# A block-sparse attention and gated FFN kernel whose instruction order is recomputed at build time: new planner prices, DMA as a planned resource, other key rows, mask rows by copies

## The chip, the cores and the metric

The kernel runs on one core of one Trainium2 chip. The metric is the time of one execution on the device in microseconds (us). A time is compared with a time, a profile with a profile; the profile's span is the time from the first to the last instruction.

## The reference

Attention over 4 batches, 8 heads, 768 positions and a head size of 64, with a mask on blocks of 32 positions, then an FFN with a three-tap convolution as gate:

```python
scores = scale * np.matmul(q, k.transpose(0, 1, 3, 2))
# visible: neighbouring blocks, first and last block row and column, 3 sampled key blocks per query block
scores = np.where(mask, scores, -1000000000.0)
attn = softmax(scores)                      # written out in the reference
x = np.matmul(attn, v)                      # (4, 768, 512) after joining the heads
h = np.maximum(x @ w_in, 0.0)               # (4, 768, 1024)
conv_out[s] = sum(conv_w[k] * h[s + k - 1] for k in range(3))
out = (h / (1.0 + np.exp(-conv_out))) @ w_out
```

The sampled blocks are an input, so all blocks are computed and the mask comes in as 24 more rows of the contraction: the query side holds a large negative number for each block that it may not see, the key side holds a one for the block that it belongs to. The softmax takes no maximum; the sum comes from a column of ones beside v.

## The kernel before, in words

**Units.** The 32 heads are 16 pairs P, four to a batch. The queries of a batch are cut in two halves, so there are 8 halves n. A half of four pairs is 18 *units* of eight 128x128 score blocks: TensorE fills one score tile `st` (L578), ScalarE takes the exponential into `pt` (L587), TensorE multiplies by v into `av` (L610). After a pair's last unit VectorE normalizes into `xtok` (L541, L542) and SyncE issues a DMA transpose into `xT` (L550). 144 units in all.

**FFN.** For each half: eight FFN1 blocks (L671, four matmuls of 384 columns into a `mix` tile), each followed by a relu into `hE` (VectorE L683 or ScalarE L681); for every two blocks GpSimd copies the edges for the taps (L696 to L702), VectorE makes three products (L710) in three slots of `m` and two sums (L718), ScalarE the tanh (L731), VectorE adds one (L734) and forms the gate `gT` (L737). Three out blocks (L640, eight matmuls of 512 columns) follow, each with an eviction into `o2s` (L650) and a store. The last column of a batch's first half waits for the second half and is patched in (L749 to L755).

**Loads.** Pair 0 comes by SyncE in fp32 (L286, staged in `o2s`) and is cast by VectorE (L474). All other q and k loads (`qk_loads`, L413) and all v loads (`v_load`, L428) are cast by the DMA and issued by GpSimd (POOL), with rows of three positions, 768 bytes; the two weight matrices are one load each (L393, L395). Pairs below `NPE = 4` are transposed by TensorE (L450) and copied out of PSUM by VectorE (L458) into the slots `et` and `ot`; the others by SyncE's DMA transposes from `nat` (L493), with an SBUF copy `ot<-et` and a mask copy `et<-msk` behind. There are six slots, three `nat` buffers and two `vn` buffers. The mask rows are built once: GpSimd forms block indicators (`bblk`, L312, L315), VectorE the visibility table from the sampled blocks (L320 to L335), TensorE multiplies the two (L344, L345); SyncE copies the rows to the other slots (L286). The conv weights come by three strided loads (L388).

**The order.** Nothing above is issued in program order. Every step is an `Op` with a price for each engine that may run it, its dependencies, buffers, and a due time made from `T(u)`, the planned start of unit u. `Scheduler.run` repeatedly takes the op that can start first (ties by due time) and puts it on its engine; the order so found is emitted, and each engine then runs its own list in order, waiting on semaphores. A DMA has a constant latency (2 to 3.8 us, the weights 12 and 14) and takes no other DMA's time. `FLEX = 1.0` keeps a relu or an eviction on VectorE unless VectorE would be a microsecond later than ScalarE. FFN work of half n is due from `T(18 (n + 1)) + 5`, its out blocks from 0.75 of a half later.

Of the kernel before, what the change touches and what calls it, by code (L numbers as in the profile page):

```python
# [48 lines left out]
FLEX = 1.0  # L49
LAT = {"PE": 0.22, "ACT": 0.20, "DVE": 0.15, "POOL": 0.20, "SP": 0.0}  # L50


class Scheduler:
# [21 lines left out]
    def run(self):  # L75
        free = {"PE": 0.0, "ACT": 0.0, "DVE": 0.0, "POOL": 0.0, "SP": 0.0}
# [10 lines left out]
        while left:  # L87
            still = []
            for o in blocked:
                r = o.earliest  # L90
                ok = True
                for d in o.deps:
                    r = max(r, d.end + (self.out_lat(d) if d.eng not in o.alts or len(o.alts) > 1
                                        or d.lat is not None else 0.0))
# [62 lines left out]
def kernel(  # L157
# [11 lines left out]
    nc = tc.nc  # L169
# [10 lines left out]
    NPE = 4  # L180
# [19 lines left out]
    NVN = 2  # L200
    vn_t = many(NVN, [128, 4, 192], BF16, "vn")
    NNAT = 3
    nat_t = many(NNAT, [128, 2, 2, 2, 192], BF16, "nat")
    MSK = sb.tile([88, 2, 2, 3, 128], BF16, tag="msk", name="msk")
    NPT = 5
    pt_t = many(NPT, [128, 1024], BF16, "pt")
    NXK = 3
    xtok_t = many(NXK, [128, 3, 2, 64], BF16, "xtok")
    rcp_t = many(NXK, [128, 2, 3], FP32, "rcp")
    NXT = 3  # L210
    xT_t = many(NXT, [128, NFC, 384], BF16, "xT")
    NHE = 3
    hE_t = many(NHE, [128, NFFC, 640], BF16, "hE")
    NCV = 3
    m_t = many(NCV, [128, 3, 2, 384], BF16, "m")
    tn_t = many(NCV, [128, 2, 384], BF16, "tn")
    NGT = 3
# [4 lines left out]
    NOS = 4  # L222
    o2s_t = many(NOS, [128, DM], FP32, "o2s")
    qf = [o2s_t[x][:, 0:384].rearrange("p (g c) -> p g c", g=2) for x in range(4)]
    winb = sb.tile([128, NFC, DFF], BF16, tag="winb", name="winb")
    woutb = sb.tile([128, NFFC, DM], BF16, tag="woutb", name="woutb")
    cw0 = sb.tile([128, 3, NFFC], FP32, tag="cw0", name="cw0")
    cw = sb.tile([128, 3, NFFC], FP32, tag="cw", name="cw")
    ident = sb.tile([128, 128], BF16, tag="ident", name="ident")
    warm = sb.tile([128, 512], BF16, tag="warm", name="warm")  # L230
    bblk = sb.tile([NB, 6, 128], BF16, tag="bblk", name="bblk")
    sbi = sb.tile([NB, 6], I32, tag="sbi", name="sbi")
# [19 lines left out]
    def t_act(n):  # L252
        return 0.147 + n / 1200.0

    def t_dps(n):
        return 0.14 + n / 960.0

    def t_d4(n):
        return 0.08 + n / 3840.0

    def t_d2(n):
        return 0.08 + n / 1920.0


    T0, PACE0, PACE1 = 7.0, 1.03, 1.2
# [3 lines left out]


    op = sc.op
    w0 = op({"DVE": 0.3}, lambda e: nc.vector.memset(warm, 0.0), -10)
    i_mem = op({"DVE": 0.1}, lambda e: nc.vector.memset(ident, 0.0), -9)
    b_mem = op({"DVE": 0.25}, lambda e: nc.vector.memset(bblk, 1.0), -9)
    a_mem = op({"DVE": 0.1}, lambda e: nc.vector.memset(A, 1.0), -8)
    r_mem = op({"DVE": 0.1}, lambda e: nc.vector.memset(row23, 1.0), -8)

    def warm_mm(e):
        nc.tensor.matmul(out=mix_t[1], lhsT=warm[:, 0:128], rhs=warm, start=True, stop=True)

    last = w0
    for x in range(7):
        last = op({"PE": 0.43}, warm_mm, -10, [last])

    def dma_h(dst, src):
        return lambda e: nc.sync.dma_start(out=dst, in_=src)  # L286

    def nat_src(t, b, h):
        return t[b, h].rearrange("(g p c) d -> p g (c d)", g=2, p=128)

    hw_q0 = op({"SP": 0.45}, dma_h(qf[0], nat_src(q, 0, 0)), -10, lat=2.2)
    hw_k0 = op({"SP": 0.45}, dma_h(qf[1], nat_src(k, 0, 0)), -9, lat=2.2)
    sb_ld = op({"SP": 0.45}, lambda e: nc.sync.dma_start(out=sbi, in_=sampled_blocks.bitcast(I32)),
               -8.5, lat=2.0)
    hw_q1 = op({"SP": 0.45}, dma_h(qf[2], nat_src(q, 0, 1)), -8, lat=2.5)
    hw_k1 = op({"SP": 0.45}, dma_h(qf[3], nat_src(k, 0, 1)), -8, lat=2.5)

    i_sel = op({"POOL": 0.3}, lambda e: nc.gpsimd.affine_select(
        out=ident, in_=ident, compare_op=ALU.not_equal, fill=1.0, base=0,
        pattern=[[-1, 128]], channel_multiplier=1), -9, [i_mem])  # L300
    col = op({"POOL": 0.2}, lambda e: nc.gpsimd.iota(colidx_i, pattern=[[1, NB]], base=0,
                                                      channel_multiplier=0), -8.9)
    a1 = op({"POOL": 0.24}, lambda e: nc.gpsimd.affine_select(
        out=A, in_=A, compare_op=ALU.is_ge, fill=0.0, base=1, pattern=[[-1, NB]],
        channel_multiplier=1), -8.8, [a_mem])
    a2 = op({"POOL": 0.24}, lambda e: nc.gpsimd.affine_select(
        out=A, in_=A, compare_op=ALU.is_ge, fill=0.0, base=1, pattern=[[1, NB]],
        channel_multiplier=-1), -8.7, [a1])
    r1 = op({"POOL": 0.24}, lambda e: nc.gpsimd.affine_select(
        out=row23, in_=row23, compare_op=ALU.is_ge, fill=0.0, base=-(NB - 1), pattern=[[0, NB]],  # L310
        channel_multiplier=1), -8.6, [r_mem])
    b1 = op({"POOL": 0.83}, lambda e: nc.gpsimd.affine_select(  # L312
        out=bblk, in_=bblk, compare_op=ALU.is_ge, fill=0.0, base=0,
        pattern=[[384, 2], [1, 3], [3, 128]], channel_multiplier=-32), -8.5, [b_mem])
# [10 lines left out]
    a3 = op({"DVE": 0.5}, a_edges, -7, [a2, r1])  # L325
    c1 = op({"DVE": 0.15}, lambda e: nc.vector.tensor_copy(out=colidx, in_=colidx_i), -7, [col])
# [11 lines left out]
    a4 = op({"DVE": 1.0}, a_rand, -9.5, [a3, c1, sb_ld])  # L338
# [3 lines left out]
    def w24(e):  # L342
        w = st_t[b_w.index]
        nc.tensor.matmul(out=w[0:NB, 0:384], lhsT=aadd, rhs=bblk[:, 0:6:2, :], start=True, stop=True)  # L344
        nc.tensor.matmul(out=w[0:NB, 512:896], lhsT=aadd, rhs=bblk[:, 1:6:2, :], start=True, stop=True)  # L345

    wmm = op({"PE": 0.7}, w24, -9, [a4, b2], alloc=b_w)

    def q_rows(dst, off):
        def fn(e):  # L350
            w = st_t[b_w.index]
            nc.scalar.copy(out=dst[64:88, 0, 0].rearrange("p c s -> p (c s)"),
                           in_=w[0:NB, off:off + 384])
        return fn

    qm_e = op({"ACT": 0.47}, q_rows(ET[0], 0), -9, [wmm], uses=[b_w])
    qm_o = op({"ACT": 0.47}, q_rows(OT[0], 512), -8.9, [wmm], uses=[b_w])

    def k_rows(dst, par):
        return lambda e: nc.vector.tensor_copy(  # L360
            out=dst[64:88, 1], in_=bblk[:, par:6:2, :].unsqueeze(1).broadcast_to([NB, 2, 3, 128]))

    km_e = op({"DVE": 0.3}, k_rows(ET[0], 0), -7.5, [b2])
    km_o = op({"DVE": 0.3}, k_rows(OT[0], 1), -7.5, [b2])
    qm_e1 = op({"DVE": 0.2}, lambda e: nc.vector.tensor_copy(out=ET[0][64:88, 0, 1], in_=ET[0][64:88, 0, 0]),
               T(0), [qm_e])
    qm_o1 = op({"DVE": 0.2}, lambda e: nc.vector.tensor_copy(out=OT[0][64:88, 0, 1], in_=OT[0][64:88, 0, 0]),
               T(0), [qm_o])
    msk = op({"DVE": 0.5}, lambda e: nc.vector.tensor_copy(out=MSK[64:88], in_=ET[0][64:88]),
             T(2), [qm_e1, km_e])  # L370
    o_mask, e_mask = {0: qm_o1}, {0: qm_e1}
    for s in range(1, NSLOT):
        if s < NPE:
            e_mask[s] = op({"SP": 0.45}, dma_h(ET[s][64:88], ET[0][64:88]), T(0) + s, [qm_e1, km_e], lat=2.0)
        o_mask[s] = op({"SP": 0.45}, dma_h(OT[s][64:88], OT[0][64:88]), T(0) + s, [qm_o1, km_o], lat=2.0)

    v_one = {}
    for s in range(NSLOT):
        v_one[s] = op({"DVE": 0.1}, lambda e, s=s: nc.vector.memset(VT[s][:, :, :, 64:65], 1.0), -5 + s)
    he_z = {}  # L380
    for s in range(NHE):
        def z(e, s=s):
            nc.vector.memset(hE_t[s][:, :, 639:640], 0.0)
        he_z[s] = op({"DVE": 0.2}, z, T(2))

    def cw_ld(e):
        for kk in range(3):
            nc.sync.dma_start(out=cw0[:, kk, :], in_=moe_conv_w[kk].rearrange("(ffc p) -> p ffc", p=128))  # L388

    cwl = op({"SP": 1.5}, cw_ld, T(8), lat=4.0, earliest=T(7))  # L390
    cw_op = op({"DVE": 0.1}, lambda e: nc.vector.tensor_scalar(out=cw, in0=cw0, scalar1=2.0, scalar2=None,
                                                                op0=ALU.mult), T(14), [cwl])
    win_ld = op({"POOL": 0.85}, lambda e: nc.gpsimd.dma_start(  # L393
        out=winb, in_=moe_w_in.rearrange("(fc p) ff -> p fc ff", p=128)), T(6), lat=12.0)
    wout_ld = op({"POOL": 0.85}, lambda e: nc.gpsimd.dma_start(  # L395
        out=woutb, in_=moe_w_out.rearrange("(ffc p) o -> p ffc o", p=128)), T(9), lat=14.0)


    first_u = [18 * (2 * (P // 4)) + (P % 4) * 4.5 for P in range(NP)]
    slot_b = [Buf(P_slot) for _ in range(NP)]  # L400
    slot_first = {}
    qk_ready = {}
    v_ready = {}

    def qk_loads(P):
# [401 lines left out]
```

## Time and profile before

| what | before |
|---|---|
| runs, us | 279.02, 275.28, 278.64; median 278.64 |
| the profiled execution, us | 277.88 |
| its span, us | 276.2 |
| its mean granted TensorE clock | 0.91 |
| TensorE busy, us | 213.5 |
| VectorE busy, us | 201.4 |
| ScalarE busy, us | 168.9 |
| GpSimd busy, us | 72.1 |
| DMA | 67778 packets, 30.35 MB |

How to read it: PE is TensorE, DVE VectorE, ACT ScalarE, POOL GpSimd, SP SyncE; "q" behind a name is the engine's queue or sequencer. A busy figure is a union of instruction durations; matmuls overlap, so their pitch is read from the start times of neighbours. A row of groups reads: line, engine, operation, out<-in with shapes, count | busy us, mean ns | idle time before it and what ended it. A row of waits reads: who <- for whom: us in total, times, longest. A row of the timeline: start, us, engine, line, operation, count, idle time before and its releaser. A row of windows: stretch, length, then busy us and instructions of PE, weight loads, DVE, ACT and POOL, granted clock, DMA share (1.00 is 16 engines busy; queues overlap, so it may be more) and GB/s.

### The profile page before, as it was taken

The page shows a single profiled execution, that of the slowest core. Times are in us where ns is not written, and L with a number is a line of the kernel's source. Part 1 is how long each engine was busy: PE and PEld are TensorE (multiplying, and loading weights), DVE is VectorE, ACT ScalarE, POOL GpSimd, SP SyncE. Part 2 cuts the span into 40 slices and gives each one's busy share as a digit, 9 for nine tenths or more (in the row PEclk, how much of TensorE's full clock was granted, in tenths as well). Part 3 has the DMA queues.
Part 4 walks back from the last instruction along what each step waited for, and adds up shares of the span by engine and source line. Part 5 has one row for each costly group of instructions (what it writes and reads, how often), then busy time and mean ns, then how long its engine had stood idle before and what let it go on. Part 6 is the DMA issues. An engine that isn't in the chain of part 4 may idle for free.

```text
span 276.2 us, 6428 instructions
## 1 busy us (share of the span) xinstructions
PE 213.5 (77%) x2503; PEld 152.0 (55%) x2521; DVE 201.4 (73%) x545; ACT 168.9 (61%) x189; POOL 72.1 (26%) x171
## 2 busy tenths in 40 slices
PE   5724499459779887997779769979898799749573
PEld 1523488337657655676557545766675567524221
DVE  6713362037997998399959994999799749986984
ACT  1511289517786887387858784887788747830420
POOL 8722331211223453022434410211112002211500
PEclk9555599959999999999999999999999999986868
DMA  6999999984215999963599964722200131011003
GB/s 141 141 211 197 160 157 116 159 154 113 55 30 120 148 167 166 230 166 64 78 180 179 168 88 157 140 64 45 93 17 15 31 129 40 18 28 76 1 0 152
DMA packets 67778, 30.35 MB, mean 110 GB/s; under 512 B 60868, under 2 KB 62916, under 8 KB 67748
## 3 DMA queue, kind: packets, MB, share of 16 engines
q0 software_dynamic: 25856, 11.14, 35.7%
q1 hardware_dynamic: 41892, 18.80, 31.6%
q8 instruction: 19, 0.31, 0.5%
q14 instruction: 11, 0.09, 0.1%
HBM read 23.08 MB, written 6.29 MB: 106 GB/s over the span
## 4 chain that ended last, share of the span: by engine, by line
DVE 53%; PE 20%; DMA 16%; issue 4%; SPq 3%; POOL 2%; ACT 1%; DVEq 0%; ACTq 0%
DVE m L710 17%; DVE m L718 10%; DVE hE L683 8%; DMA vn<-in_v_dram 7%; DMA xT<-xtok 6%; DVE gT L737 6%; PE mix L671 6%; PE mix L640 6%; DVE xtok L542 4%; PE st L578 4%; DVE tn L734 4%; PE av L610 2%; DMA et<-nat 2%; SPq L493 2%; PE st L640 1%
## 5 line engine op out<-in xcount | busy, mean ns | idle before, releaser
L587 ACT ACTIVATE pt<-st 128x1024 bf16<-128x1024 f32 x144 | 140.7, 1025 | 69.2 <-PE st L578 68.7
L671 PE MATMUL mix<-xT,winb 128*128 128x384 bf16 x256 | 53.9, 341 | 13.5 <-DMA xT<-xtok 8.6
L610 PE MATMUL av<-vt,pt 128*128 128x65 bf16 x1152 | 60.0, 195 | 0.2 <-ACT pt L587 0.2
L610 PEld LDWEIGHTS <-pt 128*128 128x128 bf16 x1152 | 52.4, 99 | 12.5 <-issue 8.7
L640 PE MATMUL mix<-woutb,gT 128*128 128x512 bf16 x143 | 41.8, 386 | 19.6 <-DVE gT L737 14.3
L710 DVE TENSOR_SCALAR m<-hE,cw 128x384 bf16<-128x384 bf16 x192 | 56.3, 348 | 0.3 <-POOL hE L702 0.3
L683 DVE TENSOR_SCALAR hE<-mix 128x384 bf16<-128x384 f32 x58 | 32.0, 552 | 26.8 <-PE mix L671 26.4
L578 PE MATMUL st<-et,ot 88*128 88x128 bf16 (+1 forms) x224 | 43.9, 240 | 1.3 <-ACT pt L587 0.9
L578 PE MATMUL st<-ot 88*128 88x128 bf16 (+1 forms) x224 | 43.6, 238 | 0.7 <-ACT pt L587 0.5
L578 PE MATMUL st<-et 88*128 88x128 bf16 (+1 forms) x208 | 43.4, 249 | 0.9 <-ACT pt L587 0.2
L578 PE MATMUL st<-ot,et 88*128 88x128 bf16 (+1 forms) x208 | 42.8, 246 | 1.5 <-ACT pt L587 0.7
L578 PEld LDWEIGHTS <-ot 88*128 88x128 bf16 x448 | 35.9, 100 | 13.6 <-issue 3.5
L696 POOL COPY hE<-hE 128x254 bf16<-128x254 bf16 x32 | 13.3, 415 | 111.3 <-DVE hE L683 93.8
L578 PEld LDWEIGHTS <-et 88*128 88x128 bf16 x416 | 33.4, 100 | 11.6 <-issue 2.9
L640 PEld LDWEIGHTS <-gT 128*128 128x128 bf16 x192 | 15.9, 101 | 42.6 <-DVE gT L737 25.5
L718 DVE TENSOR_TENSOR m<-m 128x768 bf16<-128x768 bf16 x64 | 35.6, 557 | 1.0
L731 ACT ACTIVATE tn<-m 128x768 bf16<-128x768 bf16 x32 | 26.9, 840 | 14.3 <-DVE m L718 14.1
L671 PEld LDWEIGHTS <-winb 128*128 128x128 bf16 x256 | 23.7, 101 | 19.3 <-issue 9.7
L650 DVE COPY o2s<-mix 128x512 f32<-128x512 f32 x20 | 13.4, 689 | 12.5 <-PE mix L640 12.5
L737 DVE TENSOR_TENSOR gT<-tn,hE 128x768 bf16<-128x768 bf16 x32 | 18.0, 563 | 1.1
L542 DVE TENSOR_TENSOR xtok<-av,rcp 128x384 bf16<-128x384 f32 x32 | 17.8, 558 | 1.1
L413 POOL DMA_DIRECT2D nat<-in_q_dram x15 | 11.4, 757 | 26.2 <-PE mix L450 17.7
(67 smaller groups left out, 129.2 us busy)
## 6 DMA issues: line engine op xcount, KB each, us to landing
out_dram<-o2s SPq DMA_DIRECT2D x24, 256.0 KB
vn<-in_v_dram POOLq DMA_DIRECT2D x16, 192.0 KB, 5.8
nat<-in_q_dram POOLq DMA_DIRECT2D x15, 192.0 KB, 4.8
nat<-in_k_dram POOLq DMA_DIRECT2D x15, 192.0 KB, 6.2
ot<-et SPq DMA_DIRECT2D x12, 192.0 KB
winb<-in_moe_w_in_dram POOLq DMA_DIRECT2D x1, 1024.0 KB, 12.9
woutb<-in_moe_w_out_dram POOLq DMA_DIRECT2D x1, 1024.0 KB, 17.9
et<-msk SPq DMA_DIRECT2D x12, 72.0 KB
```

What stands on the lines that cost most here:

```text
L542: nc.vector.tensor_tensor(out=xtok_t[xk.index].rearrange("p c h d -> p h c d"), in0=o[:, :, :, 0:64], in1=rcp.unsqueeze(3).broadcast_to([1 ...
L578: nc.tensor.matmul(out=st[:, 128 * x:128 * (x + n_)], lhsT=QK[kc % 2][s][0:88, 1, hh, kc // 2, :], rhs=QK[par][s][0:88, 0, hh, idx:idx + n ...
L587: nc.scalar.activation(out=pt_t[ptb.index], in_=st_t[stb.index], func=AF.Exp, bias=0.0, scale=0.125)
L610: nc.tensor.matmul(out=o[:, off:off + 65], lhsT=pt_t[ptb.index][:, 128 * x:128 * x + 128], rhs=VT[P % NSLOT][:, hh, kc, 0:65], start=(y in ...
L640: nc.tensor.matmul(out=acc(0), lhsT=gT_t[gb.index][:, ffc, 128 * c:128 * c + 128], rhs=woutb[:, ffc, :], start=(ffc == 0), stop=(ffc == NF ...
L650: nc.vector.tensor_copy(out=o2s_t[ob.index], in_=acc(0))
L671: nc.tensor.matmul(out=mix_t[hb.index][:, 0:384], lhsT=winb[:, fc, 128 * ffc:128 * ffc + 128], rhs=xT_t[xt_buf[n].index][:, fc, :], start= ...
L683: nc.vector.tensor_scalar(out=dst, in0=mix_t[hb.index][:, 0:384], scalar1=0.5, scalar2=0.0, op0=ALU.mult, op1=ALU.max)
L710: nc.vector.tensor_scalar(out=m_t[cb.index][:, x, y], in0=hE_t[heb.index][:, f0 + y, 128 * x:128 * x + 384], scalar1=cw[:, x, f0 + y:f0 + ...
L718: nc.vector.tensor_tensor(out=m[:, a_], in0=m[:, a_], in1=m[:, b_], op=ALU.add)
L731: th = op({"ACT": t_act(768)}, lambda e, cb=cb: nc.scalar.activation(out=tn_t[cb.index], in_=m_t[cb.index][:, 1], func=AF.Tanh, bias=0.0, ...
L737: g2 = op({"DVE": t_d2(768)}, lambda e, cb=cb, gtb=gtb, heb=heb, f0=f0: nc.vector.tensor_tensor(out=gT_t[gtb.index][:, f0:f0 + 2, :], in0= ...
```

## The change

The same ops are planned with other prices, and some are replaced:

- *Planner.* `FLEX` is 0; a wait on the own engine's result is charged (`OWN`); a new resource `DQ` stands for the DMA engines: each planned load takes its own time on it, one after the other. All prices and due times are new. FFN work is due later (`OFF`), out blocks 1.743 halves behind their FFN1 (`F2A`).
- *Loads.* Rows of k and v hold six positions (1536 bytes), so keys are ordered `6 p + c` and a second indicator table serves the key side. Pair 0 comes by two queues (SyncE q, ScalarE k), pair 1 by SyncE in fp32, staged in `m`, and cast by VectorE. The weights come in two halves each, with due numbers 3.3, 3.4, 6.35 and 7.35 beside P, P + 0.1 and P + 0.2 for q, k and v of pair P. The buffers `nat` go from 3 to 4, `vn` from 2 to 3, `gT` from 3 to 4.
- *Mask rows* go to the other slots by VectorE copies. `NPE` is 5, so pair 4 is transposed by TensorE too.
- *Conv.* The products use two slots of `m` instead of three; the sums are in place in the first. Products, sums and gates keep their number and size. The conv weights come in one load of 24 rows, transposed by TensorE.
- *The last half.* The last pair's `xT` is made by TensorE transposes and a ScalarE copy; each FFN1 block is split after three of its four matmuls, and every second one uses an `av` tile.
- The warm-up is 16 matmuls of 256 columns instead of 7 of 512.

The core of the diff:

```diff
-FLEX = 1.0
-LAT = {"PE": 0.22, "ACT": 0.20, "DVE": 0.15, "POOL": 0.20, "SP": 0.0}
+FLEX = 0.0
+LAT = {"PE": 0.23, "ACT": 0.20, "DVE": 0.16, "POOL": 0.20, "SP": 0.0, "DQ": 1.9}
+OWN = {"PE": 0.0, "ACT": 0.12, "DVE": 0.11, "POOL": 0.10, "SP": 0.0, "DQ": 0.0}
...
-    NPE = 4
+    NPE = 5
...
-    T0, PACE0, PACE1 = 7.0, 1.03, 1.2
+    T0, PACE0, PACE1 = 6.5, 1.032, 1.0
+    OFF = 12.0
+    S_FIRST, A_FIRST, R_FIRST, N_FIRST = 2.378, -0.753, -0.066, 0.761
+    F1S, F2A, F2S = 0.054, 1.743, 0.394
...
+        return t[b, h].rearrange("(p c) d -> p (c d)", c=6)
...
+    sb_ld = op({"SP": 0.45}, lambda e: nc.sync.dma_start(out=sbi, in_=sampled_blocks.bitcast(I32)), -20, lat=2.0)
+    for x, (t, h) in enumerate([(q, 0), (k, 0), (q, 1), (k, 1)]):
+        i_ = op({"SP": 0.45} if x % 2 == 0 else {"ACT": 0.45}, dma_h(dst_of(t, stage0[x], False), src_of(t, 0, h)), -19 + x, lat=0.4)
+        hw[x] = dq(1.0 if t is q else 0.8, [i_], -20 + x)
+    for x, t in enumerate([q, k]):
+        i_ = op({"SP": 0.45}, dma_h(dst_of(t, stage1[x], True), src_of(t, 0, slice(2, 4))),
+                -10 + x, lat=0.4)
+        hw[4 + x] = dq(2.0 if t is q else 1.6, [i_], -10 + x)
...
+    def rows_to(dst, src):
+        return lambda e: nc.vector.tensor_copy(out=dst[64:88], in_=src[64:88])
     for s in range(1, NSLOT):
         if s < NPE:
-            e_mask[s] = op({"SP": 0.45}, dma_h(ET[s][64:88], ET[0][64:88]), T(0) + s, [qm_e1, km_e], lat=2.0)
-        o_mask[s] = op({"SP": 0.45}, dma_h(OT[s][64:88], OT[0][64:88]), T(0) + s, [qm_o1, km_o], lat=2.0)
+            e_mask[s] = op({"DVE": 0.48}, rows_to(ET[s], ET[0]), T(4.5 * s) - 4, [qm_e1, km_e])
+        o_mask[s] = op({"DVE": 0.48}, rows_to(OT[s], OT[0]), T(4.5 * s) - 4, [qm_o1, km_o])
...
+    def swdge(dst, src, prio, dur, deps=(), early=0.0, alloc=None, uses=()):
+        i_ = op({"POOL": 0.8}, lambda e: nc.gpsimd.dma_start(out=dst(), in_=src), prio,
+                list(deps), lat=0.6, alloc=alloc, uses=uses, earliest=early)
+        return i_, op({"DQ": dur}, None, prio, [i_], uses=(([alloc] if alloc else []) + list(uses)))
+
+    win_ld, wout_ld = [], []
+    for x in range(2):
+        win_ld.append(swdge(lambda x=x: winb[:, :, 512 * x:512 * x + 512],
+                            moe_w_in.rearrange("(fc p) ff -> p fc ff", p=128)[:, :, 512 * x:512 * x + 512],
+                            3.3 + 0.1 * x, 4.5)[1])
...
+        m1 = op({"DVE": tm}, mul(1, 0), due + 1.7, list(relus) + [cw_op], alloc=cb, uses=[heb])
+        m0 = op({"DVE": tm}, mul(0, 1), due + 2, [edge[0]], uses=[cb, heb])
+        ad1 = op({"DVE": t_d2(768)}, add, due + 2.2, [m1, m0], uses=[cb])
+        m2 = op({"DVE": tm}, mul(2, 1), due + 2.1, [edge[0], ad1], uses=[cb, heb])
+        ad2 = op({"DVE": t_d2(768)}, add, due + 2.3, [ad1, m2], uses=[cb])
...
+        base = T(18 * (n + 1)) + OFF
...
+        d2 = base + W * F2A
```

599 lines of the change are left out of this document (305 added, 294 removed).

## The prediction

> **What bounds the kernel now.** First the page: span, ScalarE's row of 40 slices, chain.
>
> ```profile
> span 276.2 us, 6428 instructions
> ...
> ACT  1511289517786887387858784887788747830420
> ...
> DVE 53%; PE 20%; DMA 16%; issue 4%; SPq 3%; POOL 2%; ACT 1%; DVEq 0%; ACTq 0%
> ```
>
> The chain names VectorE for half the span, but slices 2 to 9 tell another story: ScalarE nearly idle. So the span is three stages, and I read each by itself. Early, ScalarE's exponentials in order of time:
>
> ```profile
> 10.65 1.94 ACT L587 ACTIVATE pt<-st 128x1024 bf16<-128x1024 f32 x2 [2.46 <-PE st L578]
> ...
> 26.34 1.94 ACT L587 ACTIVATE pt<-st 128x1024 bf16<-128x1024 f32 x2 [11.25 <-PE st L578]
> 33.26 1.02 ACT L587 ACTIVATE pt<-st 128x1024 bf16<-128x1024 f32 x1 [4.98 <-PE st L578]
> 35.51 16.61 ACT L587 ACTIVATE pt<-st 128x1024 bf16<-128x1024 f32 x18 [1.22 <-PE st L578]
> 61.40 1.02 ACT L587 ACTIVATE pt<-st 128x1024 bf16<-128x1024 f32 x1 [9.29 <-PE st L578]
> ```
>
> Undisturbed, 18 exponentials take 16.61 us, 0.92 each. The 26th of 144 starts only at 61.40, after stalls of 11.25 + 4.98 + 1.22 + 9.29 = 26.7 us. The waits of 8 to 62 us, and the loads as POOL issued them, say why:
>
> ```profile
> PE mix L450 <- DMA nat<-in_k_dram: 11.8, 2, 8.1
> ...
> PE mix L671 <- DMA xT<-xtok: 6.8, 1, 6.8
> ```
>
> ```profile
> 10.49 0.75 POOL L393 DMA_DIRECT2D winb<-in_moe_w_in_dram  x1
> 11.22 1.03 POOL L413 DMA_DIRECT2D nat<-in_k_dram  x1
> 12.24 0.89 POOL L395 DMA_DIRECT2D woutb<-in_moe_w_out_dram  x1
> 13.12 0.77 POOL L413 DMA_DIRECT2D nat<-in_k_dram  x1
> ```
>
> Keys wait behind megabytes of weights that nobody needs yet, and one xT transpose came late.
>
> After 61.40 the pace is set by three engines in lockstep. TensorE's issue pitch, from a dense stretch:
>
> ```profile
> 171.33 1.02 PE L640 MATMUL mix<-woutb,gT 128*128 128x512 bf16 x4
> 172.19 0.27 PE L578 MATMUL st<-ot 88*128 88x256 bf16 x1
> ...
> 172.63 0.41 PE L610 MATMUL av<-vt,pt 128*128 128x65 bf16 x8
> 172.88 0.22 PE L578 MATMUL st<-et 88*128 88x128 bf16 x1
> ...
> 173.32 0.81 PE L671 MATMUL mix<-xT,winb 128*128 128x384 bf16 x4
> 173.97 0.40 PE L610 MATMUL av<-vt,pt 128*128 128x65 bf16 x8
> ```
>
> By start times: scores of a unit 0.44, its AV 0.25, an FFN1 block 0.65, half an out block 0.86. One half (18 units, 8 FFN1 blocks, 3 out blocks) needs 18 x 0.69 + 8 x 0.65 + 3 x 1.72 = 22.8 us of TensorE. The waits of 62 to 250 us fill the rest:
>
> ```profile
> PE mix L640 <- DVE gT L737: 14.3, 15, 2.6
> ...
> PE mix L640 <- DVE hE L683: 4.8, 8, 1.0
> PE mix L671 <- DVE hE L683: 4.8, 8, 1.0
> ...
> PE st L578 <- ACT pt L587: 2.1, 7, 0.6
> ...
> PE mix L671 <- DMA xT<-xtok: 1.8, 2, 1.3
> ```
>
> TensorE waits 14.3 + 4.8 + 4.8 + 2.1 + 1.8 = 27.8 us, nearly all for VectorE's gates and relus. By stretches:
>
> ```profile
> 15.00:35.00 20.00, 7.88 (x68) 6.59 (x69) 5.45 (x11) 3.06 (x4) 4.09 (x6) 0.50 1.43 191
> ...
> 171.00:198.00 27.00, 23.88 (x318) 17.97 (x319) 23.45 (x62) 20.53 (x23) 4.18 (x16) 1.00 0.42 95
> ...
> 250.00:276.20 26.20, 17.14 (x63) 6.91 (x62) 19.54 (x52) 5.32 (x9) 4.95 (x12) 0.76 0.16 60
> ```
>
> VectorE is 87% busy in the steady stage, ScalarE 76%. From 61.40 to the end are 214.8 us. TensorE's need in them: 119 units x 0.69 = 82, and eight halves of FFN, 8 x 10.36 = 83, together 165. The last 26.2 us hold 8 FFN1 and 4 out blocks, 12.1 us of work, so 14.1 idle. That leaves 214.8 - 165 - 27.8 - 14.1 = 7.9 us of small gaps.
>
> **The change, part by part.** *Loads.* The new order puts the weights, in halves, behind the fourth pair's q, k and v, takes the second pair by SyncE in fp32, and reads k and v in 1536-byte rows. What is each load worth?
>
> ```profile
> q0 software_dynamic: 25856, 11.14, 35.7%
> ```
>
> 25856 packets and 11.14 MB in 35.7% of 276.2, or 98.6 us. A q, k or v load of a pair writes 128 x 768 bf16, 0.197 MB, in 512 packets: 1.7 us by bytes, 1.95 by packets. A k or v load with half the packets lies between 1.0 (only packets count) and 1.7 (only bytes); I take 1.4, the middle, since no row separates them; a loss is left out, as the bytes stay the same. Pairs 0 to 3 then cost two q at 1.85, six k and v at 1.4 and four fp32 equivalents at 1.8, about 19 us from about 2. Pair 3 lands near 23 and is first used after 13.5 units at 0.95 from unit 0's start at 10, so at 23, less 3 for transposes and copies: some 3 us late.
>
> *Start.* The block table moves ahead of q on SyncE, second-queue loads on ScalarE.
>
> ```profile
> 0.00:5.00 5.00, 3.73 (x13) 1.28 (x13) 2.95 (x21) 1.28 (x1) 3.79 (x12) 1.00 0.54 111
> ```
>
> ```profile
> 1.33 0.45 SPq L286 DMA_DIRECT2D o2s<-in_k_dram  x1
> ...
> 5.22 0.16 DVE L329 CAST rf<-sbi 24x3 f32<-24x3 int32 x1 [0.63 <-DMA sbi<-in_sampled_blocks_dram]
> ```
>
> VectorE's 0.63 us wait for the table goes: 0.6 gained, bounds 0 and 1. The Trainium skill (DMA: Bandwidth & Descriptors, "Issuing engines are not separate DMA queues") says a second issuing engine saves only the issue time, the engines being the same. By the rule the second queue gives 0.45 an issue; by the 0.54 share of the first 5 us, engines half empty, up to 2.3 us. No run shows two HWDGE queues yet; neither enters the 0.6.
>
> *Mask rows and extra copies.* (The sixteen short warm-up matmuls for seven long ones, the other key order and the halved weights move bytes and idle TensorE time alone: nothing.) Eight SyncE DMAs become nine VectorE copies, pair 4 goes through TensorE (four more PSUM copies), pair 1 needs two 768-wide casts, a second table a memset.
>
> ```profile
> L458 DVE COPY ot<-mix 64x768 bf16<-64x768 bf16 x8 | 4.5, 559 | 0.2
> ...
> L474 DVE CAST nat<-o2s 128x384 bf16<-128x384 f32 x4 | 1.3, 350 | 0.0
> ...
> L274 DVE MEMSET bblk<- 24x768 bf16 x1 | 0.7, 698 | 0.1
> ```
>
> ```profile
> 11.39 0.55 DVE L369 COPY msk<-et 24x1536 bf16<-24x1536 bf16 x1
> ```
>
> 9 x 0.55 + 4 x 0.56 + 2 x 0.7 + 0.7 = 9.3 us on VectorE, before the 26th exponential or soon after. The cover is its idle time: 5.45 busy of 20 in 15 to 35. In a head cut to some 40 us the cover is thin; without it all 9.3 show. With late pair 3 and half-clock TensorE I leave 5 us of the 26.7 stalls (bounds 1 and 15).
>
> The skill's same page ("SWDGE vs HWDGE vs iDMA") adds that VectorE's two-port copies shut GpSimd out while it writes descriptors. The k issue at 11.22 took 1.03, against 0.77 for the next, as the mask copy at 11.39 ran, so the trace partly agrees: 13 copies x 0.26 = 3.4 us of POOL at most. By the rule that goes on the loads' issue, by the row it hides behind the full DMA queue; it is part of the second rival.
>
> *The conv-weight load* becomes one of 24 rows and a PE transpose; it leaves a SyncE queue where nothing waited behind it, and no term changes.
>
> *Planner.* FLEX 0 lets ScalarE take a relu or an eviction whenever VectorE would not be earlier.
>
> ```profile
> L718 DVE TENSOR_TENSOR m<-m 128x768 bf16<-128x768 bf16 x64 | 35.6, 557 | 1.0
> ...
> L683 DVE TENSOR_SCALAR hE<-mix 128x384 bf16<-128x384 f32 x58 | 32.0, 552 | 26.8 <-PE mix L671 26.4
> ...
> L650 DVE COPY o2s<-mix 128x512 f32<-128x512 f32 x20 | 13.4, 689 | 12.5 <-PE mix L640 12.5
> ...
> L681 ACT ACTIVATE hE<-mix 128x384 bf16<-128x384 f32 x6 | 2.8, 488 | 8.6 <-PE mix L671 8.4
> ```
>
> VectorE holds 32.0 + 13.4 us of these; half moved takes 23 from VectorE and adds 20 (0.488 for 0.552) to ScalarE: per half VectorE falls from 23.45 to about 20.6 and ScalarE rises from 20.53 to 23.0, both below the 24.2 (22.8 + 10 / 7) that a half then takes. The price is a new wait: behind a relu on ScalarE that waits for its FFN1 block stand the next exponentials, and behind those TensorE's AV. The out blocks are due 1.7 periods after their FFN1, so TensorE's 14.3 us wait for gates should fall to about 3 (a gate is long done), its 9.6 for relus to 4, xT's 1.8 to nothing; its wait for ScalarE may grow from 2.1 to 3. Taken: 27.8 becomes 10 (bounds 4 and 27.8), the 7.9 of gaps 7. The conv keeps two product slots, so a third product waits for the first add: nothing where another conv's products stand between, at most the add's 0.56 in each of 32 convs, 18 us and a sum of 246. I take nothing: VectorE has 3.5 us of idle time a half, and the planner now charges itself for such waits and so puts other work between.
>
> *Tail.* Deferred out blocks fill TensorE's 14.1 us of idle time, ScalarE takes relus, the last quarter of xT goes by TensorE: 14.1 becomes 5 (bounds 2 and 14).
>
> **Sum.** 26th exponential at 61.4 - 0.6 - 21.7 = 39.1; then 165 + 10 + 7 + 5 = 187; span 226.1. The profiled execution took 277.88, 1.7 over its span, so 227.8, say **228 us**. It lies 0.8 under the median of the runs shown, 278.64, which is nothing here.
>
> **Rivals.** *Head only* (0.18): VectorE stays the pace because relus do not move, and the steady waits stay; for it, VectorE's 53% of the chain; against, ScalarE's idle quarter. 277.9 - 0.6 - 21.7 = 256. *Late head* (0.17): loads stay DMA-bound at DMA share 1.43, VectorE copies collide, TensorE's gaps hold it at clock 0.50; for it, those rows; against, the weights' new place. Leftover 15 instead of 5 and 3 more in the steady stage: 241. *TensorE-bound* (0.12): waits 4, gaps 4, tail 4, leftover 1: 228 - 6 - 3 - 1 - 4 = 214. *Slower* (0.03): SyncE issues in order; if planned landing times are early, an ET transpose that waits for its load holds every xT transpose behind it, TensorE stops in FFN1, all engines follow. The price is today's 6.8 us an instance, with 11 pairs to load so: all eleven give 228 + 75 = 303; it is slower than before from eight on, 228 + 54 = 282. For it, the 6.8 us row; against it, FFN1 is due 12 us after its attention, and the wait was long once. *Nothing gained* (0.02): a new wait eats all, 278.
>
> **How the numbers follow.** Forecast 0.48 (218 to 238 of itself). Range 210 to 256: it takes in late head and TensorE-bound, half of head only; outside are the other half (0.09), the slow and null cases (0.05), below 210 (0.04). About 2% can be told from no change here: faster 0.94, same 0.03, slower 0.03.
>
> **What would show it.** Right: the 26th exponential near 39; weights landing after the fourth pair's v; L450's successor hardly waiting for DMA; a third to a half of relus and evictions on ScalarE; TensorE's waits for gates below 5; VectorE no longer half of the chain. Wrong: ScalarE stalls over 10 us in the first 40; VectorE above 90% busy in the steady stage with TensorE waiting; SyncE holding xT; a half still taking 27 us.

## The result and the profile after

| | before | after |
|---|---|---|
| runs, us | 279.02, 275.28, 278.64, 278.28; median 278.46 | 236.37, 245.49, 236.83, 243.97; median 240.4 |
| ratio to before, 95% interval | | 0.8517 (0.8406 to 0.8627) |
| the profiled execution, us | 277.88 | 236.37 |
| its span, us | 276.2 | 234.7 |
| the 26th exponential starts at, us | 61.40 | 43.85 |
| from there to the end, us | 214.8 | 190.85 |

The four times of after lie in two groups, 236 to 237 and 244 to 246, and the ratio and the differences to after below are made of the first, mean 236.6 (against 240.4 each is 3.8 us less). The interval of after's ratio alone is 3 us to either side. The forecast was 228 (210 to 256), its span 226.1; the profiled span is 8.6 us longer. The kernel won 17.55 us of the forecast 22.3 ahead of the 26th exponential, and 23.95 of the forecast 27.8 behind it.

The page of after: span, ScalarE's 40 slices, the load queue (packets, MB, share) and the chain.

```profile
span 234.7 us, 6508 instructions
...
ACT  2166998389959989799936999999999999976541
...
q0 software_dynamic: 17664, 10.75, 33.3%
...
DVE 39%; PE 31%; DMA 20%; ACT 3%; issue 3%; SPq 1%; POOL 0%; ACTq 0%; POOLq 0%
```

ScalarE's idle slices 2 to 9 are nearly gone. VectorE's part of the chain fell from 53% to 39%; that of the DMAs rose from 16% to 20%. ScalarE's exponentials of the head, in order of time (before had 61.40 in the last row):

```profile
12.03 1.94 ACT L621 ACTIVATE pt<-st 128x1024 bf16<-128x1024 f32 x2 [3.65 <-PE st L614]
14.15 1.94 ACT L621 ACTIVATE pt<-st 128x1024 bf16<-128x1024 f32 x2 [0.19 <-PE st L614]
18.48 1.97 ACT L621 ACTIVATE pt<-st 128x1024 bf16<-128x1024 f32 x2 [2.39 <-PE st L614]
21.46 6.93 ACT L621 ACTIVATE pt<-st 128x1024 bf16<-128x1024 f32 x7 [1.01 <-PE st L614]
28.83 11.11 ACT L621 ACTIVATE pt<-st 128x1024 bf16<-128x1024 f32 x12 [0.44 <-PE st L614]
43.85 1.02 ACT L621 ACTIVATE pt<-st 128x1024 bf16<-128x1024 f32 x1 [3.92 <-PE st L614]
```

The stalls for scores behind the first exponential are 0.19 + 2.39 + 1.01 + 0.44 + 3.92 = 7.95 us, where the sum of stalls before was 26.7. TensorE's waits from 43.8 us to the end:

```profile
PE mix L665 <- DMA xT<-xtok: 7.5, 3, 4.4
PE st L732 <- DVE gT L717: 1.4, 3, 0.9
PE st L614 <- ACT pt L621: 1.1, 1, 1.1
PE av L641 <- ACT pt L621: 0.5, 1, 0.5
```

In the steady stage of before (62 to 250 us) gates cost 14.3 us and relus 9.6. Now gates cost 1.4, all of it in the last 29.7 us, relus do not appear, and the landing of `xT` is the one large wait. The relus, by engine, and one stretch of the steady stage beside the tail (us, length, then busy us and instructions of PE, weight loads, VectorE, ScalarE and GpSimd, clock, DMA share, GB/s):

```profile
L678 DVE TENSOR_SCALAR hE<-mix 128x384 bf16<-128x384 f32 x30 | 16.5, 551 | 18.8 <-PE mix L665 18.6
L676 ACT ACTIVATE hE<-mix 128x384 bf16<-128x384 f32 x30 | 14.7, 504 | 3.8 <-PE mix L665 3.8
L741 ACT COPY o2s<-mix 128x512 f32<-128x512 f32 x13 | 7.7, 591 | 2.0 <-issue 1.5 <-PE mix L732 0.4
L401 DVE COPY ot<-ot 24x1536 bf16<-24x1536 bf16 x5 | 3.0, 596 | 0.1
```

```profile
151.00:178.00 27.00, 26.84 (x373) 20.82 (x373) 24.02 (x70) 26.34 (x33) 5.65 (x19) 1.00 0.42 91
...
205.00:234.70 29.70, 22.57 (x115) 10.48 (x114) 22.87 (x69) 14.87 (x28) 7.68 (x21) 0.97 0.21 80
```

From 151 to 178 TensorE is busy 26.84 of 27 us and ScalarE 26.34: little is left to win there without less work for these two.

### The profile page after: what moved, and what is told of

Read it like the earlier page. It is cut to its first block, busy times and chain, and to the rows that moved or that the text cites. A ratio compares the mean times of both kernels' runs of the same rounds, so it can differ in the third digit from the quotient of the medians.

```text
span 234.7 us, 6508 instructions
## 1 busy us (share of the span) xinstructions
PE 205.0 (87%) x2528; PEld 152.3 (65%) x2546; DVE 184.9 (79%) x518; ACT 185.4 (79%) x234; POOL 76.7 (33%) x173
## 4 chain that ended last, share of the span: by engine, by line
DVE 39%; PE 31%; DMA 20%; ACT 3%; issue 3%; SPq 1%; POOL 0%; ACTq 0%; POOLq 0%
DMA xT<-xtok 12%; PE st L614 12%; DVE m L689 12%; PE mix L665 7%; DVE m L695 6%; PE av L641 6%; PE mix L732 5%; DVE xtok L570 4%; DVE gT L717 3%; DMA o2s<-in_q_dram 3%; DVE hE L678 3%; DMA et<-nat 2%; ACT pt L621 2%; DVE tn L708 2%; DMA ot<-et 2%
## 5 line engine op out<-in xcount | busy, mean ns | idle before, releaser
L641 PE MATMUL av<-vt,pt 128*128 128x65 bf16 x1152 | 59.4, 196 | 1.2 <-ACT pt L621 0.9
L689 DVE TENSOR_SCALAR m<-hE,cw 128x384 bf16<-128x384 bf16 x192 | 57.2, 345 | 3.5 <-ACT hE L676 1.9
L665 PE MATMUL mix<-xT,winb 128*128 128x384 bf16 x240 | 48.8, 328 | 10.7 <-DMA xT<-xtok 10.5
L641 PEld LDWEIGHTS <-pt 128*128 128x128 bf16 x1152 | 51.7, 100 | 3.9 <-ACT pt L621 1.9
L768 POOL COPY hE<-hE 128x254 bf16<-128x254 bf16 x32 | 16.8, 526 | 91.5 <-ACT hE L676 43.8
L732 PE MATMUL mix<-woutb,gT 128*128 128x512 bf16 x143 | 38.9, 384 | 1.0 <-ACT o2s L741 0.4
L678 DVE TENSOR_SCALAR hE<-mix 128x384 bf16<-128x384 f32 x30 | 16.5, 551 | 18.8 <-PE mix L665 18.6
L665 PEld LDWEIGHTS <-winb 128*128 128x128 bf16 x256 | 21.8, 98 | 13.4 <-issue 3.1
L732 PEld LDWEIGHTS <-gT 128*128 128x128 bf16 x192 | 16.3, 98 | 16.9 <-DVE gT L717 2.9
L434 POOL DMA_DIRECT2D vn<-in_v_dram x16 | 11.7, 728 | 23.8 <-DVE vt L466 21.5
L676 ACT ACTIVATE hE<-mix 128x384 bf16<-128x384 f32 x30 | 14.7, 504 | 3.8 <-PE mix L665 3.8
```

Of the source, the lines that this page charges most:

```text
L641: nc.tensor.matmul(out=av_t[av_buf[(n, P % 4)].index][:, off:off + 65], lhsT=pt_t[ptb.index][:, 128 * x:128 * x + 128], rhs=VT[P % NSLOT][ ...
L665: nc.tensor.matmul(out=tiles[hb.index][:, 0:384], lhsT=winb[:, fc, 128 * ffc:128 * ffc + 128], rhs=xT_t[xt_buf[n].index][:, fc, :], start= ...
L678: nc.vector.tensor_scalar(out=dst, in0=src, scalar1=0.5, scalar2=0.0, op0=ALU.mult, op1=ALU.max)
L689: nc.vector.tensor_scalar(out=m_t[cb.index][:, slot, o0:o1], in0=src, scalar1=w, scalar2=None, op0=ALU.mult)
L732: nc.tensor.matmul(out=acc(), lhsT=gT_t[gb.index][:, ffc, 128 * c:128 * c + 128], rhs=woutb[:, ffc, :], start=(ffc == 0), stop=(ffc == NFF ...
L768: nc.gpsimd.tensor_copy(out=h[:, f0:f0 + 2, 1:128], in_=h[:, f0:f0 + 2, 384:511])
```

## The experiments

All twelve kernels compute the whole reference. Each was compared with runs of before on the same chip, whose median there was 276.5 to 277.4. "Theory" and "rival" are those of the quoted expectations.

### b_loads: the load order alone, in the old plan

```diff
-        lq = op({"POOL": 0.85}, ld(q, 0), due, alloc=nb, lat=3.8, earliest=early)
+        lq = op({"POOL": 0.85}, ld(q, 0), due, alloc=nb, lat=0.0, earliest=early)
...
-... T(6), lat=12.0)      # w_in; w_out alike
+... T(6), lat=12.0, earliest=14.0)
```

> The kernel before with its load order alone mended: k is issued right behind q, and both weight loads stand behind the fourth pair's v. Theory (the order of the loads is most of the head's gain): the 11.25 and 4.98 us stalls of the exponentials go, some 5 come back, the 26th exponential starts near 47 instead of 61.4, the steady stage is as before, time near 264. Rival (the queue is full whatever its order, only smaller packets and fewer descriptors help): the 26th exponential stays beyond 57, time over 273.

Measured 271.73, ratio 0.9739 (0.9688 to 0.9789): a sixth of what the change brings. Two rows of ScalarE and three of SyncE's queue show why:

```profile
37.95 3.77 ACT L587 ACTIVATE pt<-st 128x1024 bf16<-128x1024 f32 x4 [1.87 <-PE st L578]
55.93 1.02 ACT L587 ACTIVATE pt<-st 128x1024 bf16<-128x1024 f32 x1 [14.21 <-PE st L578]
```

```profile
17.05 9.70 SPq L388 DMA_DIRECT2D cw<-in_moe_conv_w_dram  x3
26.88 6.54 SPq L550 DMA_TRANSPOSE xT<-xtok  x2
...
39.45 6.20 SPq L493 DMA_TRANSPOSE et<-nat  x2
...
47.06 1.22 SPq L550 DMA_TRANSPOSE xT<-xtok  x1
```

25 exponentials are done by 41.7 us, ten earlier than before. Then comes a stall of 14.21 us: TensorE stands in FFN1 for two `xT` transposes, 5.77 and 5.67 us. The first was issued at 37.24, 0.3 us behind its input, but took 2.12 us to issue, and TensorE goes on only at 46.64. The second was issued at 47.06, 6.3 us behind its input: ahead of it two `et` transposes held SyncE's queue for 6.20 us. Their loads had landed at 35.38 and 38.05, so they waited for none; their issue itself took 2.82 and 3.29 us, where the median of the run is 1.27, and why is not shown. The load order moved the wait from keys to `xT`. The theory of 264 fell.

### b_loads_cw: also the conv weights out of the way

`b_loads` with the conv weights by one 24-row load and a TensorE transpose, as in after.

> The kernel before with the mended load order (which alone gave 271) and the conv weights by one load of 24 rows and a TensorE transpose instead of three strided loads. Theory (the strided load holds SyncE's queue for 8 us, 18.4 to 26.8, so that the first xT and et transposes go out late, and FFN1 then stalls 14 us on xT): the first xT transpose goes out before 24, the stall before the 26th exponential falls below 8, time near 264. Rival (the stall is made by the et transposes, which wait for their loads in the same queue): 14 us stay, time within 1% of 271.

Measured 269.25, ratio 0.9724 (0.9684 to 0.9763). SyncE's queue, then ScalarE:

```profile
21.16 6.54 SPq L553 DMA_TRANSPOSE xT<-xtok  x2
...
39.64 4.36 SPq L496 DMA_TRANSPOSE et<-nat  x2
...
45.02 1.34 SPq L553 DMA_TRANSPOSE xT<-xtok  x1
```

```profile
55.15 1.02 ACT L590 ACTIVATE pt<-st 128x1024 bf16<-128x1024 f32 x1 [15.96 <-PE st L581]
```

The first `xT` goes out 5.7 us earlier, and the stall stays; the time cannot be told from that of `b_loads`. So the 9.70 us of the strided loads were no cause. The `et` transposes ahead of `xT` in a list that SyncE issues in order are one. The longest wait of SyncE from 18 to 62 us:

```profile
SPq L496 <- DMA nat<-in_q_dram: 6.8, 1, 6.8
```

From 27.7 to 34.6 us the list stood at an `et` transpose for its load. The third `xT`, whose input was done at 30.71, went out behind it at 37.40, and TensorE waited 6.55 us for it; the fourth, 5.2 us late, cost another 6.64. The theory fell, the rival held.

### b_loads_late: also the late FFN due times

```diff
-        base = T(18 * (n + 1)) + 5
+        base = T(18 * (n + 1)) + 12
...
-    ... base + W * (0.75 + 0.12 * x) ...
+    ... base + W * (1.743 + 0.394 * x) ...
...
-    NGT = 3
+    NGT = 4
```

> The kernel before with the mended load order, FFN1 due 12 instead of 5 us behind its half, out blocks 1.743 halves behind, and a fourth gT buffer; FLEX stays 1. Theory (load order and late FFN work only together: the 14 us stall of the load-order kernel is FFN1 put too early into TensorE's list): the 26th exponential starts near 44, TensorE's waits for gates fall from 14 to below 5, time near 252. Rival (VectorE's load sets the steady pace): the head gains 15, the steady stage stays at 215 us, time near 261.

Measured 263.36, ratio 0.9527 (0.9461 to 0.9592), 8.4 us below `b_loads`. Nearly all of it comes behind the head: the 26th exponential starts at 54.93 behind a stall of 13.30, and from there it takes 206.4 us instead of 215.3. The wait of `mix` for gates falls from 13.9 to 4.6. The theory was half right: late due times pay in the steady stage, and they did not mend the head, where the same two waits for `xT` stand (5.10 and 6.64 us).

### b_flex0: relus to ScalarE, in the old plan

```diff
-FLEX = 1.0
+FLEX = 0.0
```

> The kernel before with FLEX 0 alone: relus on ScalarE go from 6 to 33, evictions from 0 to 10, nothing else is changed but the order that follows. Theory (VectorE sets the steady pace, and moved relus free it): head as before, VectorE about 180 us busy, time near 268. Rival (the steady stage waits for gates, whose order is what counts, not for VectorE's load): time within 2% of 278.

Measured 276.61, ratio 0.9971 (0.9931 to 1.001): no change. Busy times, and TensorE's first wait:

```profile
PE 214.2 (78%) x2521; PEld 154.4 (56%) x2521; DVE 183.4 (67%) x508; ACT 185.8 (68%) x226; POOL 75.8 (28%) x171
```

```profile
PE mix L640 <- DVE gT L737: 19.4, 18, 1.7
```

VectorE lost 18.0 us of 201.4 and nothing came of it. From 62 to 250 us TensorE's waits only moved: gates cost it 19.4 us instead of 14.3, relus 6.8 instead of 9.6, all four kinds together 28.6 instead of 27.8. So the out blocks did not wait for the total of VectorE's work; the chain from relu to gate, each step behind the one before it, is what fits. My theory of 268 fell.

### a_flex1: the new plan without FLEX 0

`FLEX` back to 1.0 in after.

> The changed kernel with FLEX 1 again: 12 relus on ScalarE instead of 34, 6 evictions instead of 16. Theory (moved relus are part of the steady gain): VectorE busy near 198, head unchanged, time near 246 against 237. Rival (late out blocks alone carry the steady stage): 237, within 2%.

Measured 247.29, ratio 0.8908 (0.887 to 0.8945), 10.7 over after. VectorE's busy time goes back to 199.4. Theory right: the edit that is worth nothing in the old order is worth some 10 us in the new one.

### a_ffn_early: the new plan with the old due times

```diff
-    OFF = 12.0
+    OFF = 5.0
...
-    F1S, F2A, F2S = 0.054, 1.743, 0.394
+    F1S, F2A, F2S = 0.075, 0.75, 0.12
```

> The changed kernel with the due times of the FFN as before it (FFN1 5 us behind its half, out blocks 0.75 of a half behind their FFN1). Theory (late out blocks took TensorE's waits for gates away): those waits, 1 us in the changed kernel, come back to 8 or more, xT waits grow as FFN1 comes sooner, time near 248. Rival (prices and moved relus carry it, the due times do not): within 2% of 237.

Measured 255.41, ratio 0.9186 (0.913 to 0.9241), 18.8 over after. "Old" is meant in halves of the plan, of 18 us here and 21.6 in before. The theory had the direction, and too little of it; the waits for `xT` did not grow but fell, from 10.5 to 6.4. Two of TensorE's waits come back:

```profile
PE mix L732 <- DVE gT L717: 6.1, 10, 1.9
PE st L732 <- DVE gT L717: 5.0, 1, 5.0
```

An out block that is due early meets a gate that is not done: 11.1 us of TensorE, where after has the 1.4 shown above. That is 9.7 of the 18.8; TensorE's waits for the exponentials grow too (`st`, from 1.3 to 4.8).

### a_both: both undone

> The changed kernel with FLEX 1 and the early FFN due times, so that it keeps the loads, copies, prices and buffers alone. Alone, FLEX 1 cost 10 us and early FFN 17. Theory (moved relus help only where TensorE does not wait for gates, as FLEX 0 alone gave nothing to the kernel before): near 257, little over early FFN alone. Rival (they add up): near 264.

Measured 261.9, ratio 0.946 (0.9394 to 0.9527), 25.3 over after, where the two single edits add to 10.7 + 18.8 = 29.5. It lies between theory and rival, nearer the rival: nearly additive. All the rest of the change, with these two settings as of old, is thus worth 277.4 - 261.9 = 15.5 us.

### a_start: the table ahead of the second indicator

The order of after, but with two of GpSimd's selects behind two loads, and VectorE's key rows behind its first PSUM copy:

```diff
+        for o in order:
+            if o.eng == "POOL" and o.prio == -16:
+                o.start = 6.95
+            if o.eng == "DVE" and o.prio == -9:
+                o.start = 7.57
         order.sort(key=lambda o: (o.start, o.key))
```

> The changed kernel with the two selects of the key-side table moved behind two load issues on GpSimd, and the key-row copies behind the first PSUM copy on VectorE; nothing else is reordered. Theory (VectorE's small table operations, 0.83, 0.85 and 0.73 us instead of 0.16, 0.22 and 0.17, are held up by GpSimd's selects running beside them): the last two are short again, the table is ready 1 us sooner. Whether that shows at the end: the first exponential waits for the second head's loads at 9.05, so the time is the same within 1%. Rival (these operations are slow for another reason): 0.85 and 0.73 stay.

Measured 241.75, ratio 0.8718 (0.8657 to 0.8778). VectorE's operations on the visibility table in `a_start`:

```profile
3.87 0.15 DVE L365 CAST rf<-sbi 24x3 f32<-24x3 int32 x1
4.07 0.80 DVE L366 TENSOR_TENSOR rm<-colidx,rf 24x72 f32<-24x72 f32 x1
4.91 0.17 DVE L368 TENSOR_TENSOR rmax<-rm 24x24 f32<-24x24 f32 x1
```

The table operations are fast again where no select runs beside them (below; the second, expected short, still meets one), and the table is done at 5.69 instead of 6.96, yet the first exponential starts at 12.26, not earlier. VectorE's list still holds the second head's casts, for a load that lands at 8.48, ahead of the first head's copies (the first starts at 9.08 instead of 9.70), and the key rows, moved behind that copy by this very edit, take 0.8 us back. So no gain, as expected; but a faster table with the key rows left in place was not tried. The time lies inside the spread of after's four, yet it is 5.1 us over the 236.6 and the intervals do not touch, so "the same within 1%" was missed. TensorE waits 16.3 us for `xT` instead of 10.5, 7.7 at longest and behind 100 us, where the order is that of after.

### a_xt: every half's last quarter of xT by TensorE

```diff
-        if n == NHALF - 1 and hp == 3:
+        if hp == 3:
```

> The changed kernel with the last pair's xT of every half, not only of the last, made by TensorE transposes and a ScalarE copy. Theory (what is left of the wait is the landing of the DMA transpose, 5 to 7 us where the planner says 3.5): TensorE's 10.5 us of waits for xT fall below 3, time 230 to 233. Rival (SyncE's queue holds the other three pairs' transposes too, or the copy delays the exponentials): 236 or more.

Measured 234.15 (231.24 to 237.06), ratio 0.8431 (0.8371 to 0.8491). TensorE's waits, the first and that for `xT`, and ScalarE's head:

```profile
PE st L614 <- DMA et<-msk: 3.4, 3, 2.2
...
PE mix L665 <- DMA xT<-xtok: 1.2, 1, 1.2
```

```profile
40.95 3.86 ACT L621 ACTIVATE pt<-st 128x1024 bf16<-128x1024 f32 x4 [0.31 <-PE st L614]
```

The wait for `xT` goes from 10.5 to 1.2 us, and the 26th exponential, the second of the last row, starts near 41.9 instead of 43.85. It is the best kernel of the study: all six times lie below after's median, though its interval overlaps that of after. The wait is gone, as the theory said. How much of the 2.5 us below 236.6 comes of that is not firm: in this profile the granted clock was 1.00 from 12 to 44 us, where after had 0.87, and no run tells the two apart.

### a_best: a_xt, with later `xT` in the plan and later loads of the second head

```diff
+        if x > 1:
+            hw[x].earliest = 5.2 + x / 2
...
-    xtr[(n, hp)] = op({"SP": 1.25}, tr, due - 5, [nm], lat=2.2, ...
+    xtr[(n, hp)] = op({"SP": 1.25}, tr, due - 5, [nm], lat=4.5, ...
```

> The changed kernel with xT of every half's last pair by TensorE, a planned latency of 4.5 instead of 2.2 us for the other xT transposes, and the second head's first loads planned to land at about 8 us, so that the first head's copies go ahead of its casts. Theory (the head's first 2 us are VectorE's list waiting for the second head at 9.05, the rest is xT): the first exponential near 10.8 instead of 12.0, waits for xT below 1, time near 232. Rival (with xT gone TensorE is full, so that nothing earlier shows at the end): 234, as with the xT change alone.

Measured 236.37 (236.19 to 237.18), ratio 0.8555 (0.8529 to 0.8581): worse than `a_xt`, with intervals that do not touch. The wait for `xT` fell to 0.4 us. The first exponentials:

```profile
11.68 1.94 ACT L623 ACTIVATE pt<-st 128x1024 bf16<-128x1024 f32 x2 [3.25 <-PE st L616]
21.20 1.94 ACT L623 ACTIVATE pt<-st 128x1024 bf16<-128x1024 f32 x2 [7.59 <-PE st L616]
```

The first starts at 11.68, not at the 10.8 expected, and the plan, told that the second head comes later, puts so much ahead of it that ScalarE then idles for 7.59 us. The theory missed.

### a_mask_dma and a_rows768: the two small parts

In `a_mask_dma` the nine mask copies are SyncE DMAs at the same places of the order:

```diff
-... e_mask[s] = op({"DVE": 0.48}, rows_to(ET[s], ET[0]), ...      # o_mask alike
+... e_mask[s] = op({"DVE": 0.48}, rows_dma(ET[s], ET[0]), ...     # nc.sync.dma_start
```

> The changed kernel with the nine mask-row copies issued as SyncE DMAs at the same places of the order instead of VectorE copies (planned as the copies were). Theory (the copies cost little, as VectorE is not the bound then, and the DMAs land 2 us later at a queue that also holds xT): VectorE busy 5 us less, the early exponentials 1 to 3 us later or the same, time 237 to 240. Rival (VectorE sets the head's pace): 5 us faster, 232.

Measured 237.83 (233.08 to 245.19); the spread allows no ratio. VectorE's busy time falls from 184.9 to 179.4 us, and no difference can be told from noise. The 26th exponential starts at 45.27, no sooner than in after: that fits copies that lay beside other work, and shows no more.

In `a_rows768` the k and v rows hold three positions again (and the key indicator with them).

> The changed kernel with k and v loaded in 768-byte rows as before, keys in the order of the queries. Theory (a load's time lies between bytes and packets, so the 8000 more packets cost 30 loads about 0.3 us each on the DMA engines, felt only in the head and in the landing of xT): packets near 62000, the early exponentials 1 to 2 us later, time 238 to 242. Rival (bytes alone count): the same within 1%, 237.

Measured 241.52, ratio 0.8667 (0.8614 to 0.872), with 62818 packets instead of 54626. Against after that is 4.9 us more, against its median 1.1; the intervals overlap by a hair. Within theory's band, and not firm; the 26th exponential, at 43.96, is not the 1 to 2 us later that the theory said. Here, too, the wait for `xT` is long: 14.5 us, 7.6 at most.

## Why the prediction was nearly right, point by point

*Loads and keys: right in effect, incomplete in cause.* The stalls fell from 26.7 to 7.95 us (forecast 5, bounds 1 and 15). But "weights behind the fourth pair's q, k and v" was wrong for three of the four halves: the first of `winb` was issued at 10.07, ahead of k of pair 3 at 10.82, and both of `winb` and the first of `woutb` ahead of its v at 16.27. And the load order alone gives only a sixth of the change (`b_loads`). With the old plan `et` transposes stand ahead of `xT` in SyncE's list; in `b_loads_cw` one waits there 6.8 us for its load, in `b_loads` they are slow to issue. The first is the mechanism of the rival "slower", in the head of a kernel where I did not expect it. In after, pair 4 goes through TensorE and the plan knows when a load lands, and in the head five `xT` transposes go out ahead of the first `et`, each within 0.1 us of its input (18.22 us is the stretch from the first to the end of the fifth):

```profile
22.70 18.22 SPq L591 DMA_TRANSPOSE xT<-xtok  x5
41.01 1.24 SPq L531 DMA_TRANSPOSE et<-nat  x1
```

Which of the two, pair 4 or the resource `DQ`, does more was not tried apart.

*Start: wrong sign.* Forecast 0.6 earlier, measured 12.03 against 10.65, so 1.4 later. The wait for the table did go: its first operation starts at 3.87 instead of 5.22. But beside GpSimd's selects (4 long ones instead of 2) three operations took long, and the table is done at 6.96 instead of 6.77. The larger part is the second head. Its casts stand in VectorE's list ahead of the first head's copies, as before, and its load landed by 8.04 before and lands at 9.05 now; the first copy starts at 9.70 instead of 8.60. After, then before:

```profile
3.87 0.83 DVE L360 CAST rf<-sbi 24x3 f32<-24x3 int32 x1
...
4.73 0.85 DVE L361 TENSOR_TENSOR rm<-colidx,rf 24x72 f32<-24x72 f32 x1
5.62 0.73 DVE L363 TENSOR_TENSOR rmax<-rm 24x24 f32<-24x24 f32 x1
...
9.07 0.71 DVE L508 CAST nat<-o2s 128x384 bf16<-128x384 f32 x2 [0.27 <-DMA o2s<-in_q_dram]
9.70 0.54 DVE L486 COPY et<-mix 64x768 bf16<-64x768 bf16 x1
```

```profile
7.72 0.69 DVE L474 CAST nat<-o2s 128x384 bf16<-128x384 f32 x2
...
8.60 0.54 DVE L458 COPY et<-mix 64x768 bf16<-64x768 bf16 x1
```

The step that failed is "VectorE's 0.63 us wait for the table goes: 0.6 gained". It priced the operations behind the table as they were before (0.16, 0.22, 0.17), and it took the table for what the first exponential waits for. In `a_start` the table is 1.3 us sooner and the first exponential is not.

*Mask rows and copies: right in price.* 0.55 each was taken, 0.60 and 0.56 measured. That they hide fits `a_mask_dma`, whose spread shows no more. GpSimd's load issues took 0.75 us in the mean, 0.77 before, so the copies did not slow them as a whole. The conv's two product slots cost nothing, as taken: VectorE idles 3.5 us in all ahead of its products, 3.2 of them for relus and edges.

*Relus and evictions: right in size.* 34 of 64 relus and 16 evictions run on ScalarE; VectorE went from 201.4 to 184.9 us, ScalarE from 168.9 to 185.4. What the text did not see is that this is worth nothing by itself (`b_flex0`) and some 10 us beside late out blocks (`a_flex1`).

*Steady waits: sum right by luck, parts wrong.* Taken were 3 for gates, 4 for relus, 0 for `xT`, 3 for ScalarE: 10. Measured from 43.8 us to the tail at 205: 0, 0, 7.5 and 1.6, with 0.9 of small ones: 10.0. The gates and relus fell further than I said, and that paid for `xT`. "xT's 1.8 to nothing" is the step that failed. The plan gives such a transpose 1.25 us of SyncE and 2.2 of latency; the longest wait of after shows what it takes. SyncE's queue, a step of the chain, and TensorE:

```profile
112.45 2.06 SPq L531 DMA_TRANSPOSE et<-nat  x1
114.60 1.21 SPq L591 DMA_TRANSPOSE xT<-xtok  x1
```

```profile
114.60 6.72 DMA xT<-xtok
```

```profile
121.36 0.48 PE L665 MATMUL mix<-xT,winb 128*128 128x384 bf16 x1 [4.39 <-DMA xT<-xtok]
```

The transpose is issued 0.09 us after the `et` transpose ahead of it, 1.4 us behind its input, and lands 6.72 us later; the four others of the chain took 7.12, 5.08, 6.10 and 4.15. TensorE, in order, stands for 4.39 us. The same wait lies in the head: 2.94 of the 3.92 us before the 26th exponential. `a_xt` takes these transposes off the DMA, and the waits go.

*Tail: short by 3.4.* The last 29.7 us hold nine FFN1 and nine out blocks, 9 x 0.65 + 9 x 1.72 = 21.3 us of work, so 8.4 are idle, not 5. Of these, 4.9 lie behind TensorE's last matmul, which ends at 229.8, in the last evictions and stores (4.6 before), so the forecast of 5 left nothing for the rest: waits for gates and evictions, 2.0, and 1.5 of gaps.

*The sum.* Head 43.85 for 39.1, or 4.75 more (start 2.0, stalls 2.95, the exponentials 0.2 less); waits 10.0 for 10; tail 3.4 more; gaps 190.85 - 165 - 10.0 - 8.4 = 7.45 for 7, or 0.45 more. Together 8.6. So the start, the stalls and the tail were taken too small, and of the 7.95 us of stalls 2.9 are `xT`, which the forecast had at nothing. The rival "late head" (241) is the nearest by its number, but not by its mechanism: its stall of 15 us did not come. "Head only" fell, since the steady waits went from 27.8 to 10.0; "TensorE-bound" holds from 124 to 205 us, where TensorE is busy 26.6 to 26.8 of each 27 us.

*Open.* What makes the landing of `xT` vary is not shown: with the same transposes, TensorE waited 10.5, 16.3 and 14.5 us for it in after, `a_start` and `a_rows768`. Of the 15.5 us that neither the due times nor `FLEX` bring (`a_both`), no single part was tried by itself in the new plan but the mask copies and the rows. One hardware queue instead of two for the first loads was not tried; the DMA share of the first 5 us is 0.54 in both kernels, at 111 and 134 GB/s. The Trainium skill (DMA: Bandwidth & Descriptors, "Issuing engines are not separate DMA queues") says that a second issuing engine saves issue time alone; a first exponential that came no earlier does not speak against it.

## What to carry to other kernels

When one load order frees the first stage, look at every in-order queue behind it for the next thing late: here SyncE's list turned a wait for keys into one for `xT`, and TensorE's own order passed it on to ScalarE. Taking work off a busy engine was worth nothing while TensorE waited for the end of its chain (`b_flex0`), and some 10 us once the consumer was due later (`a_flex1`, `a_ffn_early`): try such edits together. Measure how long a DMA takes to land in this kernel: the `xT` transposes took 4 to 7 us where the plan had 3.45. Telling the plan so (`a_best`, with another edit) gained nothing; taking the last transpose of each half off the DMA took the wait away.

## What was not expected of the hardware

Small VectorE operations lasted as long as a GpSimd select beside them. GpSimd's selects in after:

```profile
3.82 0.85 POOL L341 TENSOR_SCALAR_AFFINE_SELECT bblk<-bblk 24x768 bf16<-24x768 bf16 x1
4.64 0.86 POOL L341 TENSOR_SCALAR_AFFINE_SELECT bblkn<-bblkn 24x768 bf16<-24x768 bf16 x1
5.46 0.85 POOL L341 TENSOR_SCALAR_AFFINE_SELECT bblk<-bblk 24x768 bf16<-24x768 bf16 x1
```

They end at 4.67, 5.50 and 6.31; the three VectorE operations shown above, started within 0.16 us of them, end at 4.70, 5.58 and 6.35, and took 0.83, 0.85 and 0.73 us for the 0.16, 0.22 and 0.17 of before. In `a_start` the second, which starts behind a select (3.93 to 4.79), took 0.80; the first, which starts at 3.87, just ahead of it, took 0.15, and the third, behind it, 0.17. The Trainium skill (SBUF — State Buffer, "SBUF: two separate sides") states an exclusive lock of a port pair that GpSimd shares with VectorE's two-port operations, and with those of two SBUF inputs while GpSimd reads SBUF: whichever starts first holds it for the whole instruction. These rows agree, down to an operation of 72 numbers in all.

The three strided loads of the conv weights held SyncE's queue for 9.70 us in `b_loads`, the third alone for 8.36; as one load of 24 rows they are gone from that place, at no gain in time there.
